# Load order and first matmuls of a fused linear-attention and SwiGLU kernel: x in two tiles, the first weight quarter in two halves, eight DMAs more

## The chip, the cores and the metric

The kernel runs on one core of one Trainium2 chip. The metric is the device time of one execution in microseconds (us). The program drives the TensorE matmul engine (PE in the profile), VectorE (DVE), ScalarE (ACT), GpSimd (POOL) and the queue of SyncE (SP), which issues nearly every DMA.

## What is computed

The input x has 2048 tokens of 512 numbers. Two blocks read it, and a gate per token mixes their results. Cut to what matters:

```python
g = sigmoid((x * gate_w).sum(-1, keepdims=True))
q, k, v = heads(x @ wqkv)                 # 32 heads of 16
pq, pk = phi(q), phi(k)                   # phi(t) = where(t > 0, t + 1, exp(t)) + 1e-6
kv = einsum("bhsd,bhse->bhde", pk, v);  z = pk.sum over tokens
a = (pq @ kv / (pq . z + 1e-6)) @ wo
b = (silu(x @ w1) * (x @ w3)) @ w2        # 1376 hidden columns
out = g * a + (1 - g) * b
```

All inputs and the output are bf16.

## The kernel before, in words

Tokens are worked in 16 tiles of 128 (`NT`), the 512 columns of x in four quarters of 128 (`kc`, `KC` = 4). A matmul contracts over 128 partitions, so a projection of one tile is four matmuls that add up in one PSUM bank, one for each quarter kc, and each needs the quarter kc of the weight and the transposed quarter of the tile, `xT[:, kc, tile]`.

**Loads.** They are issued from SP's queue (`dq`), in the order of the code, and SP issues one at a time. First comes `x_first` (L129): the first 256 tokens in one DMA of 256 KB, with two neighbouring tokens on each partition, so that tile 0 holds the even and tile 1 the odd tokens of the 256; `store` (L508) writes the output rows of tiles 0 and 1 back in the same pattern. Then `load_wqk(kc)` (L126) runs four times: each brings one quarter of wq and wk together, 256 KB. Then `load_xT(t)` (L123) brings tiles 2 to 15 already transposed, by DMA transposes; the same tiles untransposed (L141, named `natural`) come between them, in three DMAs. After those come gate and remainder columns (L143 to L147), w1 and w3 (L150, one DMA of 1280 KB each), wv (L151), wo (L152), w2 (L154) and w2x (L156). ACT's queue issues one small DMA, `touch` (L133).

**The first two tiles.** They are transposed on TensorE, by a matmul with the identity. The order is written out by hand. `warm_step(13)` (L359) runs 13 matmuls on constants. Then six transposes (L365) make quarters 0, 1 and 2 of both tiles; DVE (L379, L381) and ACT (L380, L382) copy them from PSUM into `xT`. The projections follow (`proj_mm`, L183): for quarter 0, k of tile 0, q of tile 0, k of tile 1 and q of tile 1, each in a bank of its own (banks 4 to 7); then the last two transposes (L365) and their copy (L394); the same four matmuls for quarter 1; k of both tiles for quarters 2 and 3; q of tile 0 and of tile 1 for quarters 2 and 3.

**What follows.** `phi` (ACT L196, DVE L198 and L201) turns a bank into pq or pk. `g_step` (L231) adds pk times x into four banks over all tokens; `k_step` and `q_step` project the next tiles. The sum of pk over all tokens is kept by POOL (L215), turned by a DMA transpose (`zaT`, L421) and spread over the partitions. Then four blocks of 512 tokens run through w1 and w3 (L303, L309), and the output tiles through L475 and L492.

Of the kernel before, what the change touches and what calls it, by code (L numbers as in the profile page):

```python
# [8 lines left out]
ACT = mybir.ActivationFunctionType  # L9
# [7 lines left out]
def kernel(  # L17
# [17 lines left out]
    nc = tc.nc  # L35
    P = nc.NUM_PARTITIONS

    Bb, S, D = A_x.shape
# [3 lines left out]
    KC = D // P  # L42
# [16 lines left out]
    x2d = A_x.flatten_outer_dims()  # L59
    out2d = out.flatten_outer_dims()  # L60
    x_t = x2d.rearrange("(t p) d -> p t d", p=P)
    wqkv_r = A_wqkv.rearrange("(kc d) n -> d kc n", d=P)
    w1_r = B_w1.rearrange("(kc d) f -> d kc f", d=P)
    w3_r = B_w3.rearrange("(kc d) f -> d kc f", d=P)
# [8 lines left out]
    ident = consts.tile([P, P], BF16, name="ident")  # L73
# [6 lines left out]
        out=bmask[:], in_=bmask[:], pattern=[[-Dh, HPC], [0, Dh]], compare_op=ALU.is_ge,  # L80
# [3 lines left out]
        out=bmask[:], in_=bmask[:], pattern=[[Dh, HPC], [0, Dh]], compare_op=ALU.is_ge,  # L84
# [22 lines left out]
    xN = consts.tile([P, NT, D], BF16, name="xN")  # L107
    wqk = consts.tile([P, KC, 2 * D], BF16, name="wqk")
    wq = wqk[:, :, 0:D]
    wk = wqk[:, :, D : 2 * D]  # L110
# [3 lines left out]
    w1 = consts.tile([P, KC, F0], BF16, name="w1")  # L114
    w3 = consts.tile([P, KC, F0], BF16, name="w3")
    w2 = consts.tile([P, FC, D], BF16, name="w2")
    xT = consts.tile([P, KC, S], BF16, name="xT")
    act_pre = consts.tile([P, 1], BF16, name="act_pre")
    dq = nc.sync
# [5 lines left out]
    def load_wqk(kc):  # L125
        dq.dma_start(out=wqk[:, kc, :], in_=wqkv_r[:, kc, 0 : 2 * D])  # L126

    x_first = x2d[0 : 2 * P, :].rearrange("(p j) d -> p j d", j=2)
    dq.dma_start(out=xN[:, 0:2, :], in_=x_first)  # L129
    nc.scalar.activation(out=act_pre[:], in_=warm[:, 0:1], func=ACT.Exp)  # L130

    touch = consts.tile([P, 2, 16], BF16, name="touch")
    nc.scalar.dma_start(out=touch[:], in_=wqkv_r[:, 1:3, 0:16])  # L133
    for kc in range(KC):
        load_wqk(kc)
    natural = {3: (2, 4), 5: (4, 8), 8: (8, 16)}
    for t in range(2, NT):
# [4 lines left out]
    with nc.allow_non_contiguous_dma(reason="gate column"):  # L142
        dq.dma_start(  # L143
            out=wr[:, :, 2 * FR : NR], in_=gate_w.rearrange("(kc d o) -> d kc o", d=P, o=1)
        )
    dq.dma_start(out=wr[:, :, 0:FR], in_=w1_r[:, :, F0:F])
    dq.dma_start(out=wr[:, :, FR : 2 * FR], in_=w3_r[:, :, F0:F])  # L147
    for w, w_r, cuts in ((w1, w1_r, (0, KC)), (w3, w3_r, (0, KC))):
        for a, b in zip(cuts, cuts[1:]):
            dq.dma_start(out=w[:, a:b, :], in_=w_r[:, a:b, 0:F0])  # L150
    dq.dma_start(out=wv[:], in_=wqkv_r[:, :, 2 * D : 3 * D])  # L151
# [5 lines left out]
        out=w2x[:].rearrange("p r d -> p (r d)"),  # L157
        in_=w2x_r[None].to_broadcast([TPB, RP, RG * D]),
# [11 lines left out]
    bank = [psum.tile([P, D], FP32, name=f"bank{i}") for i in range(8)]  # L170
    turn = {"mm": 0, "ab": 0}

    def mm_tile():
        turn["mm"] += 1
        return bank[4 + (turn["mm"] - 1) % 4]
# [6 lines left out]
    def proj_mm(ps, t, w, kc):  # L182
        nc.tensor.matmul(  # L183
            ps[:], lhsT=xT[:, kc, t * P : (t + 1) * P], rhs=w[:, kc, :],
            start=(kc == 0), stop=(kc == KC - 1),
        )
# [170 lines left out]
    def warm_step(n):  # L357
        for _ in range(n):
            nc.tensor.matmul(  # L359
                bank[7][:, 0:256], lhsT=warm[:, 0:P], rhs=warm, start=True, stop=True  # L360
            )

    def transpose_block(t, kc, dst):

        nc.tensor.matmul(  # L365
            dst, lhsT=xN[:, t, kc * P : (kc + 1) * P], rhs=ident[:], start=True, stop=True
        )

    def transpose_kc(kc, ps):
        for t in range(2):  # L370
            transpose_block(t, kc, ps[:, t * P : (t + 1) * P])

    warm_step(13)

    for t in range(2):
        transpose_block(t, 0, bank[t][:, 0:P])
    transpose_kc(1, bank[2])
    transpose_kc(2, bank[3])
    nc.vector.tensor_copy(out=xT[:, 0, 0:P], in_=bank[0][:, 0:P])  # L379
    nc.scalar.activation(out=xT[:, 0, P : 2 * P], in_=bank[1][:, 0:P], func=ACT.Copy)  # L380
    nc.vector.tensor_copy(out=xT[:, 1, 0 : 2 * P], in_=bank[2][:, 0 : 2 * P])  # L381
    nc.scalar.activation(out=xT[:, 2, 0 : 2 * P], in_=bank[3][:, 0 : 2 * P], func=ACT.Copy)  # L382
    first = {(t, n): mm_tile() for n, t in (("k", 0), ("k", 1), ("q", 0), ("q", 1))}
    w_of = {"k": wk, "q": wq}

    def first_mm(n, t, kc):
        proj_mm(first[t, n], t, w_of[n], kc)

    for kc in range(2):
        for n, t in (("k", 0), ("q", 0), ("k", 1), ("q", 1)):  # L390
            first_mm(n, t, kc)
        if kc == 0:
            transpose_kc(3, bank[0])
            nc.vector.tensor_copy(out=xT[:, 3, 0 : 2 * P], in_=bank[0][:, 0 : 2 * P])  # L394
    for kc in range(2, KC):
        for t in range(2):
            first_mm("k", t, kc)
# [103 lines left out]
        )  # L501

    def store(t, o, cs=slice(0, D)):
        if t < 2:
            rows = out2d[0 : 2 * P, :].rearrange("(p j) d -> p j d", j=2)[:, t, :]
        else:
            rows = out2d[t * P : (t + 1) * P, :]
        dq.dma_start(out=rows[:, cs], in_=o[:, cs])  # L508

    def out_first(tb):  # L510

        t = tb * TPB
        b_part(t, bank[0], range(AHEAD))
        rem_out_step(tb, bank, started=(0,))
        keep = [mm_tile() for _ in range(TPB)]
        rem_out_step(tb + 1, keep, ends=True)
        rem_keep(tb + 1, keep)
        b_part(t, bank[0], range(AHEAD, FC))
        aga = a_part(t, mm_tile())
        o = work.tile([P, D], BF16, tag="o", bufs=3, name="o")  # L520
        mix(t, bank[0], aga, o)
        store(t, o)

    def out_step(tb, tt):
        t = tb * TPB + tt
        held = tb % 2 == 0
        if held and tt == 0:
            return out_first(tb)
        aga = a_part(t, mm_tile() if held else ab_tile())
        o = work.tile([P, D], BF16, tag="o", bufs=3, name="o")  # L530
        if t < NT - 1:
            b_ps = bank[tt] if held else ab_tile()
            b_part(t, b_ps, range(FC), started=held)
            mix(t, b_ps, aga, o)
            store(t, o)
            return
        for lo, hi in ((0, 2 * P), (2 * P, 3 * P), (3 * P, D)):
            cs = slice(lo, hi)
            b_ps = ab_tile()
            b_part(t, b_ps, range(FC), cs)  # L540
            mix(t, b_ps, aga, o, cs)
            if lo == 0:
                store(t, o, cs)
        store(t, o, slice(2 * P, D))
# [56 lines left out]
```

## Time and profile before

| what | value |
|---|---|
| median of 3 runs | 178.08 us (178.05 to 178.58) |
| the profiled execution: its own time | 178.0 us |
| the profiled execution: its span, first to last instruction | 176.3 us |
| TensorE's granted clock, mean | 1.000 |
| PE busy | 172.5 us, 969 matmuls |
| DVE busy | 110.4 us |
| POOL busy | 63.2 us |
| ACT busy | 59.1 us |
| DMA | 15.57 MB, mean 88 GB/s |

All times inside the execution are counted from the start of the span; 1.7 us of the execution's own time lie outside it. "Busy" counts running instructions; issuing a DMA is not busy time. Neighbouring matmuls overlap, so a matmul of 128x512 lasts 379 ns but the next one starts some 216 ns after it: rows of the timeline give a group's first start and the time until its last end. A view that follows the chain of waits back from the last instruction tells which work set the end.

### The profile page before, as it was taken

What the parts mean: (1) busy time and instruction counts of PE and PEld (TensorE: products, weight loads), DVE (VectorE), ACT (ScalarE), POOL (GpSimd) and SP (SyncE); (2) the same over time, 40 slices, a digit from 0 to 9 for tenths busy, and PEclk for the clock granted to TensorE, in tenths of its full rate; (3) what the DMA queues carried; (4) which work ended last, traced back from release to release, by engine and by line L of the source; (5) the groups of instructions that cost most, each with busy time, mean ns of one, the idle gap of its engine ahead of it and who ended that gap; (6) DMA issues with size and microseconds to landing.
All of it is one profiled execution on the core that took longest, in us unless ns stands there. A gap on an engine that the chain in (4) does not pass through costs nothing.

```text
span 176.3 us, 2685 instructions
## 1 busy us (share of the span) xinstructions
PE 172.5 (98%) x969; PEld 82.5 (47%) x969; DVE 110.4 (63%) x207; ACT 59.1 (34%) x109; POOL 63.2 (36%) x106
## 2 busy tenths in 40 slices
PE   8999999999999999999999999999999999999993
PEld 5444444444456443444444466444444444444453
DVE  1399788888764899777343477853435775344363
ACT  4354544544753443422423101134225123422000
POOL 5086657557300668486400044550000562000000
DMA  6998959995204111323200013330000233000001
GB/s 186 262 178 228 183 103 279 402 349 198 66 4 52 26 30 34 83 65 89 60 0 0 0 33 84 84 89 0 0 4 0 60 89 89 4 0 0 30 30 60
DMA packets 29232, 15.57 MB, mean 88 GB/s; under 512 B 21028, under 2 KB 27428, under 8 KB 29220
## 3 DMA queue, kind: packets, MB, share of 16 engines
q1 hardware_dynamic: 28948, 15.41, 35.3%
q8 instruction: 7, 0.11, 0.3%
q10 hardware_dynamic: 272, 0.01, 0.1%
q14 instruction: 5, 0.04, 0.1%
HBM read 8.86 MB, written 2.10 MB: 62 GB/s over the span
## 4 chain that ended last, share of the span: by engine, by line
PE 94%; DMA 2%; SPq 1%; DVE 0%; issue 0%
PE bank L492 20%; PE bank L303 20%; PE bank L309 20%; PE bank L183 15%; PE bank L231 8%; PE bank L475 8%; PE bank L245 3%; DMA wqk<-in_A_wqkv_dram 2%; PE bank L278 2%; SPq L126 1%; PE bank L447 0%; SPq L129 0%; PE bank L462 0%; DVE o L498 0%
## 5 line engine op out<-in xcount | busy, mean ns | idle before, releaser
L315 DVE TENSOR_TENSOR hT<-bank,sg 128x512 bf16<-128x512 f32 x40 | 27.3, 682 | 31.0 <-PE bank L309 30.9
L303 PE MATMUL bank<-xT,w 128*128 128x512 bf16 x160 | 41.1, 379 | 0.0
L309 PE MATMUL bank<-xT,w 128*128 128x512 bf16 x160 | 41.1, 379 | 0.0
L314 ACT ACTIVATE sg<-bank 128x512 bf16<-128x512 f32 x40 | 23.9, 597 | 45.9 <-PE bank L303 45.9
L492 PE MATMUL bank<-w,hT 128*128 128x512 bf16 (+2 forms) x180 | 37.5, 355 | 0.0
L337 POOL TENSOR_TENSOR pqs<-pq,rden 128x512 bf16<-128x512 bf16 x16 | 16.9, 1056 | 54.4 <-issue 46.9
L183 PE MATMUL bank<-wqk,xT 128*128 128x512 bf16 x128 | 30.8, 381 | 0.1
L215 POOL TENSOR_TENSOR zacc<-zacc,pk 128x128 f32<-128x128 f32 x56 | 23.3, 446 | 10.4 <-DVE pk L201 10.4
L492 PEld LDWEIGHTS <-hT 128*128 128x128 bf16 x180 | 16.7, 98 | 18.4 <-issue 0.8
L309 PEld LDWEIGHTS <-w 128*128 128x128 bf16 x160 | 15.7, 98 | 18.9
L303 PEld LDWEIGHTS <-w 128*128 128x128 bf16 x160 | 15.5, 98 | 18.2 <-issue 0.2
L498 DVE SCALAR_TENSOR_TENSOR o<-bank,omg_all,aga 128x512 bf16<-128x512 f32 (+2 forms) x18 | 12.5, 692 | 14.6 <-PE bank L492 11.7
L183 PEld LDWEIGHTS <-xT 128*128 128x128 bf16 x128 | 12.4, 98 | 15.2 <-issue 0.7
L322 POOL TENSOR_TENSOR pr<-pq,zb 128x512 f32<-128x512 bf16 x16 | 18.4, 1154 | 0.1
L231 PE MATMUL bank<-pk,xN 128*128 128x512 bf16 x64 | 16.4, 379 | 0.0
L475 PE MATMUL bank<-M,pqT 128*128 128x512 bf16 x64 | 16.1, 379 | 0.0
L196 ACT ACTIVATE eq<-bank 128x512 bf16<-128x512 f32 x16 | 9.4, 597 | 16.0 <-PE bank L183 16.0
L201 DVE SCALAR_TENSOR_TENSOR pk<-bank,emk 128x512 bf16<-128x512 f32 x16 | 11.1, 692 | 1.6
L196 ACT ACTIVATE ek<-bank 128x512 bf16<-128x512 f32 x16 | 9.4, 597 | 6.7 <-PE bank L183 6.7
L201 DVE SCALAR_TENSOR_TENSOR pq<-bank,emq 128x512 bf16<-128x512 f32 x16 | 11.1, 692 | 0.5
L326 DVE TENSOR_REDUCE den<-pr 128x32 f32<-128x512 f32 x16 | 10.8, 676 | 0.0
L231 PEld LDWEIGHTS <-xN 128*128 128x128 bf16 x64 | 6.3, 98 | 7.6
(54 smaller groups left out, 95.7 us busy)
## 6 DMA issues: line engine op xcount, KB each, us to landing
w<-in_B_w_dram SPq DMA_DIRECT2D x3, 1280.0 KB, 10.2
out_dram<-o SPq DMA_DIRECT2D x15, 128.0 KB, 1.9
wqk<-in_A_wqkv_dram SPq DMA_DIRECT2D x4, 256.0 KB, 3.7
xN<-in_A_x_dram SPq DMA_DIRECT2D x1, 1024.0 KB
xN<-in_A_x_dram SPq DMA_DIRECT2D x2, 256.0 KB, 2.8
xN<-in_A_x_dram SPq DMA_DIRECT2D x1, 512.0 KB, 4.7
wv<-in_A_wqkv_dram SPq DMA_DIRECT2D x1, 512.0 KB, 11.2
wo<-in_A_wo_dram SPq DMA_DIRECT2D x1, 512.0 KB, 12.1
```

The costliest lines, as they stand in the source:

```text
L183: nc.tensor.matmul(ps[:], lhsT=xT[:, kc, t * P : (t + 1) * P], rhs=w[:, kc, :], start=(kc == 0), stop=(kc == KC - 1),)
L196: nc.scalar.activation(out=e[:], in_=ps[:], func=ACT.Exp)
L201: nc.vector.scalar_tensor_tensor(out=dst, in0=ps[:], scalar=0.0, in1=em[:], op0=ALU.max, op1=ALU.add)
L215: nc.gpsimd.tensor_tensor(out=(zaccb if t == NT - 1 else zacc)[:, cs], in0=zacc[:, cs], in1=pk[t][:, cs], op=ALU.add,)
L231: nc.tensor.matmul(bank[kc][:], lhsT=xN[:, t, kc * P : (kc + 1) * P], rhs=pk[t][:], start=(t == 0), stop=(t == NT - 1),)
L303: nc.tensor.matmul(g_ps[:], lhsT=w1[:, kc, fs], rhs=xT[:, kc, tok], start=(kc == 0), stop=(kc == KC - 1),)
L309: nc.tensor.matmul(u_ps[:], lhsT=w3[:, kc, fs], rhs=xT[:, kc, tok], start=(kc == 0), stop=(kc == KC - 1),)
L314: nc.scalar.activation(out=sg[:], in_=g_ps[:], func=ACT.Silu)
L315: nc.vector.tensor_tensor(out=hT[tb][:, fc, :], in0=u_ps[:], in1=sg[:], op=ALU.mult)
L322: nc.gpsimd.tensor_tensor(out=pr[t][:], in0=pq[:, t, :], in1=zb[:], op=ALU.mult)
L475: nc.tensor.matmul(ps[:], lhsT=pqT[:, c, ts], rhs=M2[:, c, :], start=(c == 0), stop=(c == KC - 1),)
L492: nc.tensor.matmul(ps[:, 0 : cs.stop - cs.start], lhsT=hT[tb][:, fc, tt * P : (tt + 1) * P], rhs=w2[:, fc, cs], start=(fc == 0 and not sta ...
```

## The change

x's first 256 tokens come in two DMAs of 128 KB, tile 0 being the first 128 tokens and tile 1 the next, and the first quarter of the weights in two, wk and wq; the issue order is x tile 0, wk's quarter 0, x tile 1, wq's quarter 0, then the joined quarters 1, 2 and 3 as before. w1 and w3 come in four DMAs each in place of one. These are eight DMAs more: one for x, one for the weight quarter, six for w1 and w3. There are 10 warm-up matmuls in place of 13. All four quarters of tile 0 are transposed first, one to a bank, and copied by DVE and ACT in turn in four copies; k of tile 0 for quarter 0 follows; then tile 1 is transposed into the same four banks and copied in the same way; then k of tile 1, q of tile 0 and q of tile 1 for quarter 0. Quarter 1 is projected in the order k 0, q 0, k 1, q 1; the rest has its order unchanged. The output rows of tiles 0 and 1 are stored as all others are.

```diff
-    x_first = x2d[0 : 2 * P, :].rearrange("(p j) d -> p j d", j=2)
-    dq.dma_start(out=xN[:, 0:2, :], in_=x_first)
+    def load_x(t):
+        dq.dma_start(out=xN[:, t, :], in_=x_t[:, t, :])
+
+    load_x(0)
...
-    for kc in range(KC):
+    dq.dma_start(out=wk[:, 0, :], in_=wqkv_r[:, 0, D : 2 * D])
+    load_x(1)
+    dq.dma_start(out=wq[:, 0, :], in_=wqkv_r[:, 0, 0:D])
+    for kc in range(1, KC):
         load_wqk(kc)
...
-    for w, w_r, cuts in ((w1, w1_r, (0, KC)), (w3, w3_r, (0, KC))):
+    for w, w_r, cuts in ((w1, w1_r, range(KC + 1)), (w3, w3_r, range(KC + 1))):
         for a, b in zip(cuts, cuts[1:]):
             dq.dma_start(out=w[:, a:b, :], in_=w_r[:, a:b, 0:F0])
...
-    def transpose_block(t, kc, dst):
...
-    def transpose_kc(kc, ps):
...
-    warm_step(13)
-
-    for t in range(2):
-        transpose_block(t, 0, bank[t][:, 0:P])
-    transpose_kc(1, bank[2])
-    transpose_kc(2, bank[3])
...
+    def transpose_tile(t):
+
+        ts = slice(t * P, (t + 1) * P)
+        for kc in range(KC):
+            nc.tensor.matmul(
+                bank[kc][:, 0:P], lhsT=xN[:, t, kc * P : (kc + 1) * P], rhs=ident[:],
+                start=True, stop=True,
+            )
+        for kc in range(KC):
+            if kc % 2 == 0:
+                nc.vector.tensor_copy(out=xT[:, kc, ts], in_=bank[kc][:, 0:P])
+            else:
+                nc.scalar.activation(out=xT[:, kc, ts], in_=bank[kc][:, 0:P], func=ACT.Copy)
+
+    warm_step(10)
+    transpose_tile(0)
...
-    for kc in range(2):
-        for n, t in (("k", 0), ("q", 0), ("k", 1), ("q", 1)):
-            first_mm(n, t, kc)
-        if kc == 0:
-            transpose_kc(3, bank[0])
-            nc.vector.tensor_copy(out=xT[:, 3, 0 : 2 * P], in_=bank[0][:, 0 : 2 * P])
+    first_mm("k", 0, 0)
+    transpose_tile(1)
+    for n, t in (("k", 1), ("q", 0), ("q", 1)):
+        first_mm(n, t, 0)
+    for n, t in (("k", 0), ("q", 0), ("k", 1), ("q", 1)):
+        first_mm(n, t, 1)
...
-        if t < 2:
-            rows = out2d[0 : 2 * P, :].rearrange("(p j) d -> p j d", j=2)[:, t, :]
-        else:
-            rows = out2d[t * P : (t + 1) * P, :]
-        dq.dma_start(out=rows[:, cs], in_=o[:, cs])
+        dq.dma_start(out=out2d[t * P : (t + 1) * P, cs], in_=o[:, cs])
```

More of the change, by code (lines that the diff above doesn't have):

```diff
@@ L361, in warm_step @@
             )
-    def transpose_block(t, kc, dst):
-        nc.tensor.matmul(
-            dst, lhsT=xN[:, t, kc * P : (kc + 1) * P], rhs=ident[:], start=True, stop=True
-        )
-    def transpose_kc(kc, ps):
-        for t in range(2):
-            transpose_block(t, kc, ps[:, t * P : (t + 1) * P])
-    warm_step(13)
-    for t in range(2):
-        transpose_block(t, 0, bank[t][:, 0:P])
-    transpose_kc(1, bank[2])
-    transpose_kc(2, bank[3])
[L379 to L382, printed above, removed]
+    def transpose_tile(t):
[12 more added lines that the diff above has]
+    transpose_tile(0)
     first = {(t, n): mm_tile() for n, t in (("k", 0), ("k", 1), ("q", 0), ("q", 1))}
```

## The prediction, made before the changed kernel ran

> **What bounds the kernel now.** I read part 1 of the page first. PE is busy for 172.5 of 176.3 us, so the time is PE's work plus the few places where PE waits.
>
> ```profile
> PE 172.5 (98%) x969; PEld 82.5 (47%) x969; DVE 110.4 (63%) x207; ACT 59.1 (34%) x109; POOL 63.2 (36%) x106
> ```
>
> Next comes the chain of work that ended last, in order of time (start, duration, what). Everything the change touches lies in its first 8 us.
>
> ```profile
> 0.80 0.39 SPq L129
> ...
> 2.19 0.43 SPq L126
> 2.62 0.04 issue
> 2.66 4.38 DMA wqk<-in_A_wqkv_dram
> 7.04 0.04 issue
> 7.08 2.32 PE bank L183 x10
> ```
>
> The chain does not run through x or the transposes. It runs through SP, which issues x and four weight quarters one after another, then through the landing of the fourth quarter at 7.04 us, and from 7.08 through PE to the end. What PE does before 7.08 counts only if it lasts beyond the landing. The timeline of the first 9 us, PE's rows and the weight loads' (PEld), shows how near it is:
>
> ```profile
> 0.84 2.93 PE L359 MATMUL bank<-const-bfloat16-1.0 128*128 128x256 bf16 x13 [0.84 <-PEq L585]
> 3.57 0.84 PE L365 MATMUL bank<-ident,xN 128*128 128x128 bf16 x6
> 3.92 0.29 DVE L379 CAST xT<-bank 128x128 bf16<-128x128 f32 x1 [3.92 <-PE bank L365]
> 4.26 1.26 PE L183 MATMUL bank<-wqk,xT 128*128 128x512 bf16 x4
> 5.36 0.28 PE L365 MATMUL bank<-ident,xN 128*128 128x128 bf16 x2
> 5.47 3.93 PE L183 MATMUL bank<-wqk,xT 128*128 128x512 bf16 x16
> 7.08 1.82 PEld L183 LDWEIGHTS <-xT 128*128 128x128 bf16 x9 [0.41 <-issue]
> ```
>
> Quarter 0 and all transposes are through at 5.47. Six matmuls follow at 0.216 us (an eight-matmul piece of the chain lasts 1.73 us): four for quarter 1, two for quarter 2. They would end at 6.77. The weight loads then stand still for 0.41 us until 7.08. So PE has some 0.3 us of slack before quarter 3, and no more than that can be won there.
>
> **The change, part by part.** The sum is made against the profiled execution's own 178.0 us (span 176.3); the median of the runs shown, 178.08, is 0.08 above it.
>
> *PE's start.* x's first tile is half the bytes of the old first load. That load landed 2.6 us after its issue (DMA issues of the profile), at 3.4. Half of it, 131 thousand bytes at the 335 GB/s quoted below, is 0.39 us, so tile 0 lands near 3.0. Ten warm-up matmuls end there too: 2.93/13 = 0.225 us each from 0.84 gives 3.1. Four transposes at some 0.11 us start there (say 3.05); the first copy starts 0.35 later (3.57 to 3.92 before) and lasts 0.29, and 0.05 passes to the matmul: 3.74, half a microsecond before the old 4.26. It takes 0.40 there (the first matmul of L183 started at 4.26, the second at 4.66), so tile 1's transposes run from 4.14 to 4.6, its first copy ends 0.64 after 4.14, and k of tile 1 starts near 4.83. Three matmuls at 0.216 end quarter 0 at 5.48, where it was 5.47. The early start is spent on a second round of transpose, copy and wait. Quarters 1 and 2 end at 6.78: nothing gained, nothing lost. The cover is quarter 3's landing. Without it each 0.1 us here would cost 0.1 us. The copies are two more (eight for six), on DVE and ACT, which have nothing else to do before 7.49.
>
> *The issue order.* SP's queue has these rows:
>
> ```profile
> 1.25 1.84 SPq L126 DMA_DIRECT2D wqk<-in_A_wqkv_dram  x4
> 3.14 2.59 SPq L123 DMA_TRANSPOSE xT<-in_A_x_dram  x2
> ```
>
> Four issues take 3.14 - 1.25 = 1.89, or 0.47 us each. Two more stand ahead of quarter 3, which is now issued at 2.66 + 0.94 = 3.60. What that does to the landing is the one term that counts, and the trace before cannot show it. Its ends: nothing, if the queue is full and the bytes alone decide, since x and the four quarters have the same 1.31 MB; +0.94, if the 4.38 us from issue to landing stays. Between them stands the rate of the transfers. Two stretches, the first of nearly only 2 KB packets (3.0 to 5.3 us), the second of 1 KB packets alone (11.0 to 11.9 us), columns packets, MB, share of 16 engines:
>
> ```profile
> DMA packets 451, 0.77 MB, mean 335 GB/s; under 512 B 75, under 2 KB 75, under 8 KB 451
> q1 hardware_dynamic: 421, 0.77, 102.9%
> ```
>
> ```profile
> q1 hardware_dynamic: 313, 0.32, 102.7%
> ```
>
> A 2 KB packet took 1.029 x 16 x 2.3/376 = 0.101 us of an engine (451 less the 75 small ones are 376), a 1 KB packet 1.027 x 16 x 0.9/313 = 0.047. Splitting rows costs nothing per byte. But a 128 KB load at every 0.47 us asks for 279 GB/s only, less than the 335 that the engines deliver: the first four loads now run at SP's pace, not the engines'. Data begin some 1.2 us after an issue (0.80 to about 2.0, where the DMA row of the first 9 us leaves zero). Quarter 1, issued at 2.66, therefore starts at 3.86, and the 786 thousand bytes of quarters 1 to 3 take 2.35 us at 335 GB/s, to 6.21. Before, 1.31 MB from 2.0 took to 5.91. That is +0.30. At 402 GB/s, the highest slice of the page, it is 3.86 + 1.96 = 5.82 against 5.26, or +0.56. I take the middle, **+0.43**, because the landing at 7.04 lies 1.1 us behind the flow's end, so some engines run late, and nothing shows that the new pauses absorb their lateness.
>
> *Behind quarter 3.* Tile 2's transposed load is issued 0.94 later too. It landed 4.4 us after 3.14, at 7.5, and its first matmul is PE's at 8.37 (six matmuls after 7.08). With the whole 0.94 it lands at 8.5, when PE would need it at 8.80: covered by 0.3. Tile 3 is needed 1.5 us later. POOL has no DMA in this queue.
>
> *w1 and w3 in quarters.* Six more issues of 0.51 us (L150) plus the 0.94 make SP 4.0 us later behind them; w2x, the last load, was issued by 36.6, and SP then waited 9.6 us for POOL's zaccb (SP's own waits) before it issued zaT at 46.4. The 5.6 us left cover it. w1 and w3 landed by 36.8, with first use at 46.5; wv by 38.3, first use 53.0. Price nothing; without the cover, up to 4.0 us. The stores keep their number and sizes: nothing.
>
> *Sum.* PE's start 0, issue order +0.43, the rest 0: 178.0 + 0.43 = 178.4, against the median 178.08 + 0.43 = **178.5 us**. Allowing the neighbourhood of the two rates, this case reaches from +0.2 to +0.7. A measurement of this kernel tells 0.3%, or 0.53 us, from no change: the case straddles that line.
>
> **The rivals.**
>
> *The landing goes by the issue, +0.7 to +0.94 (178.8 to 179.0).* For it: the first transposed load also landed 4.4 us after its issue, as quarter 3 did. Against it: the four quarters took 2.9, 3.2, 4.1 and 4.4, growing as a queue does.
>
> *The landing is no later, and PE moves up.* If what delayed quarter 3 was contention, with the transposes right behind it, a later issue of these and calmer first loads may bring it back to 7.04 or earlier. PE can use it to 6.8 only: -0.3 to +0.2, 177.8 to 178.3. For it: the 1.1 us between flow and landing. Against it: the fewer bytes in flight early on.
>
> *PE's clock comes up later (the slow side).* The page gives a mean granted clock of 1.000, but the rows show two speeds: six transposes in 0.84 us at 3.57, two in 0.28 at 5.36; matmuls 0.40 apart at 4.26, 0.216 from 4.93. The step follows some 4 us of unbroken PE work. The new order breaks it twice, each time from the end of four transposes to the first copied quarter, by 0.26 us. If that puts the step off until after quarter 2, nine matmuls (three, four, two) run at 0.43 from 4.83 and end at 8.7 instead of 7.08: +1.6, 179.7. It decides from a step later than about 6.8 us; earlier, the wait for quarter 3 hides it. Against it: PE stays busy for 87% of the time from 0.84 to 4.83 (0.52 of 3.99 idle), and 13 warm-ups or 10 plus transposes fill the same stretch. [...]
>
> **How the numbers follow.** Forecast 0.42 (0.27 within the line, 0.15 over it); landing by issue 0.24, all slower; landing no later 0.22, of which 0.04 are faster by over 0.3% and 0.18 within; late clock 0.10 slower; 0.02 for something else, slower. Faster 0.04, same 0.45, slower 0.51. The range 177.8 to 179.2 takes in the first three cases and leaves the late clock and the tails out; the forecast's own is 178.3 to 178.8.
>
> **What would show it.** In the profile after: SP issues quarter 3 near 3.6; its landing between 7.2 and 7.7, with PE's first matmul behind it and the idle time before it grown from 0.41 to 0.8 or so; the first projection at 3.7 and quarter 0 through near 5.5; no wait from there to the end, w1's first use included. A landing at 7.0 or before, a matmul spacing of 0.43 beyond 5 us, or a wait before tile 2's projection would each prove a step wrong.

## The result, and the profile after

The changed kernel takes 179.28 us (median of 18 runs, 178.57 to 180.79) and the kernel before 178.24 us (18 runs beside them, 177.66 to 178.90): a ratio of 1.0069, 95% interval 1.0048 to 1.0090. It is slower, by 1.0 us, more than the 0.4 forecast and just outside the range.

The profiled execution of the changed kernel lasts 178.86 us, 0.86 above that of before (178.0). Its span is 176.8, only 0.5 longer. So the loss has two parts, one inside the span and one outside. The chain of waits in order of time (start, duration, what), for the changed kernel:

```profile
0.80 0.39 SPq L129
...
2.67 0.43 SPq L126
3.10 0.04 issue
3.14 0.43 SPq L126
3.57 0.04 issue
3.61 3.95 DMA wqk<-in_A_wqkv_dram
7.57 0.04 issue
7.61 2.32 PE bank L188 x10
```

It has the shape it had before. SP issues seven loads in place of five, quarter 3 goes out at 3.61 instead of 2.66, lands at 7.57 instead of 7.04, and PE's dense stretch starts at 7.61 instead of 7.08: 0.53 later. From there on nothing changes. The issue of zaT, for instance, stands at 46.88 instead of 46.35, again 0.53 later. PE's rows in the timeline:

```profile
3.08 0.61 PE L372 MATMUL bank<-ident,xN 128*128 128x128 bf16 x4
3.76 0.61 PE L188 MATMUL bank<-wqk,xT 128*128 128x512 bf16 x1
4.16 0.63 PE L372 MATMUL bank<-ident,xN 128*128 128x128 bf16 x4
4.86 2.55 PE L188 MATMUL bank<-wqk,xT 128*128 128x512 bf16 x9
7.61 2.10 PE L188 MATMUL bank<-wqk,xT 128*128 128x512 bf16 x9 [0.20 <-DMA wqk<-in_A_wqkv_dram]
```

The first projection does start half a microsecond earlier (3.76 for 4.26). Then PE waits for tile 1's copy until 4.86. Inside the row of nine matmuls it also waits for quarter 2, which lands at 6.78 (the seventh of them ends near 6.5, the next starts at 6.82), and behind that row it waits for quarter 3.

The other 0.34 us lie outside the span: an execution's own time minus its span is 1.7 us before and 2.05 here, and it hardly varies within a kernel. The span does vary. Over the 18 runs it was 176.5 to 177.5 in thirteen and 178.0 to 178.7 in five, while the kernel before had 175.8 to 177.2 in all of its 72 runs whose span is known. The experiments take these three apart: the later landing, the long executions, and the time outside.

### The profile page after: what moved, and what is told of

It reads as the page before. It is cut to its first block, busy times and chain, and to the rows that moved or that the text cites. A ratio compares the mean times of both kernels' runs of the same rounds, so it can differ in the third digit from the quotient of the medians.

```text
span 176.8 us, 2672 instructions
## 1 busy us (share of the span) xinstructions
PE 171.5 (97%) x949; PEld 82.1 (46%) x966; DVE 109.8 (62%) x208; ACT 59.5 (34%) x111; POOL 63.2 (36%) x106
## 4 chain that ended last, share of the span: by engine, by line
PE 93%; DMA 2%; SPq 1%; issue 1%; DVE 0%
PE bank L308 20%; PE bank L493 20%; PE bank L314 19%; PE bank L188 15%; PE bank L236 8%; PE bank L476 8%; PE bank L250 3%; DMA wqk<-in_A_wqkv_dram 2%; PE bank L283 2%; SPq L126 0%; SPq L129 0%; PE bank L448 0%; SPq L138 0%; SPq L136 0%; PE bank L463 0%
## 5 line engine op out<-in xcount | busy, mean ns | idle before, releaser
L308 PE MATMUL bank<-xT,w 128*128 128x512 bf16 x158 | 40.8, 379 | 0.2
L314 PE MATMUL bank<-xT,w 128*128 128x512 bf16 x156 | 40.4, 379 | 0.1
L493 PE MATMUL bank<-w,hT 128*128 128x512 bf16 (+2 forms) x176 | 37.0, 355 | 0.5 <-issue 0.3
L476 PE MATMUL bank<-M,pqT 128*128 128x512 bf16 x61 | 15.6, 379 | 0.1
```

What stands on the lines that cost most here:

```text
L308: nc.tensor.matmul(g_ps[:], lhsT=w1[:, kc, fs], rhs=xT[:, kc, tok], start=(kc == 0), stop=(kc == KC - 1),)
L314: nc.tensor.matmul(u_ps[:], lhsT=w3[:, kc, fs], rhs=xT[:, kc, tok], start=(kc == 0), stop=(kc == KC - 1),)
L476: nc.tensor.matmul(ps[:], lhsT=pqT[:, c, ts], rhs=M2[:, c, :], start=(c == 0), stop=(c == KC - 1),)
L493: nc.tensor.matmul(ps[:, 0 : cs.stop - cs.start], lhsT=hT[tb][:, fc, tt * P : (tt + 1) * P], rhs=w2[:, fc, cs], start=(fc == 0 and not sta ...
```

## Experiments

Each kernel ran several times, with the kernel before on the same chip beside it. "Outside" is the median of time minus span, "ACT" and "DVE" the number of their instructions in part 1 of the page, "long" the runs whose span was over 177.9. The runs of the kernel before came in four sets, each beside some of the variants; their median span was 176.6 in three sets and 176.8 in the one beside the two queues, the two small loads, the two ACT more and the copies on DVE.

| kernel | time minus before, us | ratio, 95% interval | span, median | long | ACT / DVE | outside |
|---|---|---|---|---|---|---|
| before (72 runs) | | | 176.6 | 0 of 72 | 109 / 207 | 1.71 |
| changed | +1.04 | 1.0048 to 1.0090 | 177.2 | 5 of 18 | 111 / 208 | 2.05 |
| loads alone | +1.11 | 1.0061 to 1.0126 | 177.65 | 2 of 6 | 109 / 207 | 1.70 |
| changed, w1 and w3 whole | +1.17 | 1.0054 to 1.0110 | 177.4 | 2 of 6 | 111 / 208 | 2.04 |
| PE order alone | +0.47 | 1.0010 to 1.0035 | 176.7 | 0 of 12 | 111 / 208 | 2.04 |
| w1 and w3 in pieces alone | +0.21 | 1.0003 to 1.0032 | 176.8 | 0 of 12 | 109 / 207 | 1.70 |
| changed, two queues | +0.46 | 1.0022 to 1.0089 | 177.3 | 2 of 5 | 111 / 208 | 1.71 |
| before, two small loads | +0.67 | 1.0028 to 1.0121 | 177.5 | 2 of 5 | 109 / 207 | 1.71 |
| before, two ACT more | +0.39 | 1.0007 to 1.0040 | 176.9 | 0 of 5 | 111 / 207 | 2.03 |
| changed, copies on DVE | +0.42 | 1.0013 to 1.0070 | 177.1 | 1 of 5 | 109 / 210 | 1.86 |
| changed, two ACT more | +0.92 | 1.0046 to 1.0107 | 177.5 | 3 of 9 | 113 / 208 | 1.73 |
| changed, fillers | +1.14 | 1.0046 to 1.0084 | 177.35 | 0 of 6 | 111 / 208 | 2.04 |
| before, later need | +0.03 | 0.9984 to 1.0017 | 176.6 | 0 of 12 | 109 / 207 | 1.72 |
| before, few warm-ups | +1.04 | 1.0043 to 1.0093 | 177.6 | 2 of 7 | 109 / 207 | 1.71 |
| changed, fillers and two ACT | +0.60 | 1.0012 to 1.0042 | 177.2 | 0 of 8 | 113 / 208 | 1.73 |
| before, four ACT more | +0.15 | 1.0005 to 1.0025 | 176.8 | 0 of 9 | 113 / 207 | 1.71 |

### Which part carries what

**Loads alone.** The kernel before with the diff's edits to the loads of x and wqk and to the stores.

> The kernel before, with the new loads of x and of the first weight quarter in the new order, and the plain stores; 13 warm-ups, the old order of transposes and matmuls, w1 and w3 whole. Pacing theory (two more issues of 0.47 us on SP delay quarter 3 whatever PE does): quarter 3 lands near 7.57 us as in the changed kernel, PE's first matmul behind it starts near 7.6, the span is 0.5 us longer than before, 176.8. Rival, the new order on PE is what costs: landing may be late, but the span stays within 0.2 of 176.3 or the time does not move. Outside the span (1.7 us before, 2.05 in the changed kernel): if it grows with the number of DMAs, 2 more give about +0.1, so 178.8 to 178.9 in all; if it comes from the pieces of w1 and w3, it stays at 1.7.

The span grew by 1.05, more than expected, and the time outside stayed at 1.70. The chain of waits of this kernel:

```profile
3.62 4.54 DMA wqk<-in_A_wqkv_dram
8.16 0.04 issue
8.20 2.32 PE bank L188 x10
```

Quarter 3 landed at 8.16. The old order on PE is still there, so the loss inside the span belongs to the loads, and so do long runs. The stores, which this kernel changes too, are not the cause: 1.13 of the 1.3 us between the two profiled spans are there when zaT is issued (47.48 for 46.35), before the first store.

**PE order alone.** The diff's edits to transposes and first matmuls on the kernel before, with 13 warm-ups.

> The kernel before with the new order on PE alone (tile by tile transposes, eight copies, the new order of quarter 0), 13 warm-ups, the old loads and stores. Pacing theory: quarter 3 is issued at 2.66 and lands near 7.04 as before; PE starts from x at 3.4 instead of 3.0, so its own work to quarter 2 ends some 0.4 to 0.6 later than in the changed kernel, near 7.3 to 7.5, and now PE itself decides: span 0.2 to 0.5 above 176.3. Rival, late clock: in some runs one to two us more, as in five of the eighteen runs of the changed kernel (180.05 to 180.79). Outside the span 1.7 in both.

Quarter 3 landed at 6.92, and the chain shows that PE itself was the later of the two:

```profile
4.47 0.58 PE bank L183
5.06 0.10 PE bank L367
5.16 0.02 issue
5.18 0.30 DVE xT L373
5.49 0.05 issue
5.53 4.28 PE bank L183 x19
```

After the copy of tile 1's first quarter, nineteen matmuls run without a gap, through the place where quarter 3 is first needed. The span's median moved by 0.1 only, and no run was long; 0.33 of the loss of 0.47 is the time outside, 2.04.

**w1 and w3, both ways.** In the changed kernel:

```diff
-    for w, w_r, cuts in ((w1, w1_r, range(KC + 1)), (w3, w3_r, range(KC + 1))):
+    for w, w_r, cuts in ((w1, w1_r, (0, KC)), (w3, w3_r, (0, KC))):
```

and the reverse in the kernel before.

> The changed kernel with w1 and w3 loaded whole again, six DMAs fewer. Theory of a price for each DMA outside the span: time outside falls from 2.05 to about 1.8, the span stays at 176.8 to 177.0, the median falls by 0.25 to about 179.0. Pacing theory alone: no change, 179.3, since those loads are 9 us ahead of their first use. Rival, the pieces of w1 and w3 disturb the stream (a later landing, a slower z chain): the span itself falls.

> The kernel before with w1 and w3 in four loads each and nothing else. Price for each DMA outside the span: span 176.3 as before, time outside 1.7 + 0.25, median 0.2 to 0.3 above before. If nothing is paid for an issued DMA: median as before within 0.1. Rival, pieces disturb the stream: the span grows, by a wait at the first use of w1 or of the transposed z.

The price for each DMA falls: six more leave 1.70, six fewer leave 2.04. Undoing the pieces won nothing; making them cost 0.2, which is at the edge of what the runs can tell (0.05 to 0.6). In the profiled execution of that kernel 0.44 us of delay stand already at 9.84 (9.40 before), behind a wait for quarter 1 that landed at 6.09, while its first load of w1 is issued at 25.6; so that much, at least, is not the pieces' doing.

### The landing of quarter 3

**Two queues.** The changed kernel with

```diff
-    load_x(1)
-    dq.dma_start(out=wq[:, 0, :], in_=wqkv_r[:, 0, 0:D])
+    nc.scalar.dma_start(out=xN[:, 1, :], in_=x_t[:, 1, :])
+    nc.scalar.dma_start(out=wq[:, 0, :], in_=wqkv_r[:, 0, 0:D])
```

> The changed kernel, with x tile 1 and wq's quarter 0 issued from ACT's queue, where SP's issues do not wait for them: quarter 3 is again issued near 2.67. Landing goes by issue (some 4.4 us after it, whatever stands in the queue): landing near 7.1 instead of 7.6 to 8.1, span near 176.6 at the median (177.2 in the changed kernel). Flow theory (bytes at the engines' rate): the same bytes, no pauses between them, landing as before, also near 7.1. Rival, the smaller pieces themselves are slow (1 KB rows, more landings), wherever they are issued: span stays at 177.2 or more. Outside the span 2.05 as in the changed kernel if it goes with ACT's or PE's program.

Quarter 3, issued at 2.67, landed at 7.25, as expected. But the span did not come back (177.3, beside 176.8): in the profiled run, a long one, PE waited for wq's quarter 0 instead, which ACT's queue brought at 6.25, as the chain of waits shows (the three shorter runs, 177.1 to 177.3, have no profile):

```profile
1.85 4.40 DMA wqk<-in_A_wqkv_dram
6.25 0.04 issue
6.29 5.41 PE bank L188 x18
```

**Two small loads.** The kernel before with

```diff
+    small = consts.tile([P, 2, 16], BF16, name="small")
     for kc in range(KC):
+        if kc < 2:
+            dq.dma_start(out=small[:, kc, :], in_=wqkv_r[:, 3, kc * 16 : (kc + 1) * 16])
         load_wqk(kc)
```

> The kernel before, with two loads of 4 KB more on SP's queue, one ahead of quarter 0 and one ahead of quarter 1; nothing reads them. The same bytes of x and weights, in the old pieces, but quarter 3 is issued near 3.6. Landing goes by issue: landing near 8.0, span up by about 0.9 to 177.5. Flow theory: +0.3 to +0.56, span 176.9 to 177.1. Rival, the pieces are what costs (1 KB rows, splitting of x): nothing but the 4 KB, span 176.6 as before. Outside the span 1.70 in each case.

8 KB that nothing reads made the span 0.3 to 0.7 longer in the three shorter runs (177.1, 177.3, 177.5, beside a median of 176.8) and two of five long. So two issues ahead of quarter 3 are enough to cost span; smaller rows or more tiles are not needed to explain that. The size, 0.5 in the middle run, is nearer to the flow theory's +0.3 to +0.56 than to the +0.9 of a landing that goes by the issue, and the one profiled landing, 7.64, settles nothing: without the small loads, in the kernel with two ACT more beside it, quarter 3 landed at 7.62. Each of the two loads of 4 KB took as long on SP as a load of 256 KB, some 0.47 us: the first 0.41 and 0.05 to the next issue, the first quarter of the kernel before 0.42 and 0.05.

Put together: where quarter 3 was issued near 3.61, it landed at 7.57, 7.63, 7.64, 8.01, 8.07, 8.15, 8.15, 8.16, 8.27 and 8.29 in ten profiled executions, median 8.1. Where it was issued at 2.67, at 6.50, 6.92, 6.94, 7.04, 7.25, 7.48, 7.62 and 8.05, median 7.15. The medians differ by 0.95 and the means by 0.77, with an interval of some 0.4 to 1.2, since landings of one order spread so widely. The span moved less: in runs that are not long it lies 0.4 above that of the kernel before for the changed kernel, 0.25 to 0.75 for its variants, and 1.0 for loads alone.

Two more things stand in these eighteen traces. First, quarter 3 lands 0.67 to 0.79 us behind quarter 2 in every one, although it is issued 0.47 behind it; so what delays quarter 3 is there in quarter 2 already, and in five executions (w1 and w3 in pieces, two ACT more, four ACT more, copies on DVE, and one of the changed kernel) the chain runs through quarter 1, whose landing at 6.09 to 6.64 sets the start of sixteen matmuls. Second, a trace records sixteen completions for each load, and the load has landed with the last. With the old order in seven executions and the new one in nine (the two queues and the two small loads left aside), quarter 2's first completion came at 5.21 to 5.60 and at 5.79 to 6.06, medians 5.46 and 5.87: 0.41 later, although the issue is 0.95 later. Its last completion came 0.3 to 2.0 us behind the first with the old order (median 1.1) and 1.0 to 1.8 with the new one (median 1.5). So by these medians the first data of quarter 2 came 0.41 later, and the rest of the landing's move is a longer tail of late completions.

### The long executions

The two small loads' profiled execution is a long one (span 179.4). PE's rows:

```profile
3.57 0.84 PE L368 MATMUL bank<-ident,xN 128*128 128x128 bf16 x6
5.50 1.86 PE L186 MATMUL bank<-wqk,xT 128*128 128x512 bf16 x4 [1.09 <-DMA wqk<-in_A_wqkv_dram]
7.16 0.42 PE L368 MATMUL bank<-ident,xN 128*128 128x128 bf16 x2
7.38 4.34 PE L186 MATMUL bank<-wqk,xT 128*128 128x512 bf16 x13
```

PE stood idle for 1.09 us until quarter 0 came at 5.46. Four matmuls then take 1.86 where they took 1.26 before: they start 0.43 apart, and this lasts until 9.9, while quarter 3 had landed at 7.64. The clock's step is here, as in the prediction, the place where the spacing of matmuls falls from some 0.43 us (half speed) to 0.216 (full speed). The granted clock reads 1.00 on both sides of it (3.50 to 4.60 and 4.95 to 7.00 us of the kernel before), so that a clock is the cause is the author's reading and was not shown. In this execution the step came late, and PE, not the load, set the end. The profiled execution of two queues is a late clock too: after 6.29, matmuls start 0.43 apart until 8.80. PE's wait before that row was shorter, 0.48 us, behind one of 0.23 at 4.52.

```profile
6.29 3.04 PE L188 MATMUL bank<-wqk,xT 128*128 128x512 bf16 x7 [0.48 <-DMA wqk<-in_A_wqkv_dram]
```

A wait does not always do it. In loads alone PE waited 0.63 us for x's second tile, and the transposes behind that wait ran at full speed (they start 0.06 apart, where those at 3.57 in the kernel before start 0.11 apart):

```profile
4.52 0.45 PE L370 MATMUL bank<-ident,xN 128*128 128x128 bf16 x5 [0.63 <-DMA xN<-in_A_x_dram]
```

**Few warm-ups.** The kernel before with `warm_step(3)` for `warm_step(13)`; no load is touched.

> The kernel before with 3 warm-up matmuls in place of 13, so that PE is idle from about 1.5 to 3.45 us; the loads are untouched. Clock theory: full speed comes only after some 4 us of unbroken work, so not before about 7.5 to 8; transposes and the matmuls of quarters 0 and 1 run at half speed (0.43 apart), quarter 2 ends near 9.5, span 1.5 to 2.5 us longer, 178 to 179. Rival, the clock takes little notice of a pause of 2 us: step near 5, span 176.6 as before.

```profile
0.84 0.80 PE L359 MATMUL bank<-const-bfloat16-1.0 128*128 128x256 bf16 x3 [0.84 <-PEq L585]
3.59 0.82 PE L365 MATMUL bank<-ident,xN 128*128 128x128 bf16 x6 [1.94 <-DMA xN<-in_A_x_dram]
4.37 1.86 PE L183 MATMUL bank<-wqk,xT 128*128 128x512 bf16 x4
```

The same 1.86, after an idle stretch of 1.94 us; matmuls start 0.43 apart until 9.66, although quarter 3 landed early, at 6.50. Time +1.04. The size varies from run to run (spans 177.2 to 178.5), and five of seven are below what was expected.

**Fillers.** The changed kernel with

```diff
     transpose_tile(0)
+    warm_step(1)
...
     first_mm("k", 0, 0)
+    warm_step(2)
     transpose_tile(1)
-    for n, t in (("k", 1), ("q", 0), ("q", 1)):
+    warm_step(1)
+    first_mm("k", 1, 0)
+    warm_step(2)
+    for n, t in (("q", 0), ("q", 1)):
         first_mm(n, t, 0)
```

> The changed kernel with six more warm-up matmuls in the places where PE waits for a copy or a piece in quarter 0 (one behind each tile's transposes, two ahead of tile 1's, two behind k of tile 1). Clock theory (the runs of more than 178 us span come from a wait of PE of about a microsecond for a late piece, after which PE stays at half speed until 9 to 10 us): PE stays busy, no run above 177.8, median span near 177.0. Rival (those runs are late landings of quarter 3 as such): one run in four above 178 as before. The fillers take at most 6 x 0.21 us of PE ahead of a landing that comes 0.5 us after PE is ready, so a small loss is possible in the other runs: up to 0.4.

No run of six was long, nor one of eight in the kernel with fillers below. The changed kernel and all variants with the new loads, or two extra issues, and without fillers had 17 long runs in 54. The median span (177.35) did not fall: the landing still decides it.

**The changed kernel again, twice.** A single execution each.

> The changed kernel once more, for a profile of a run above 178 us of span (5 of 18 were). Clock theory: in such a run PE's matmuls are 0.43 us apart until 9 to 10 us, after a wait of about a microsecond for a late piece of quarter 0 or 1; span 178.0 to 178.7. Rival: matmuls 0.216 apart from 5 us on and a landing of quarter 3 near 9. A run below 178 should show the clock's step near 5 and a landing between 7.2 and 8.3.

> As the run before, a second execution of the changed kernel: late clock with matmuls 0.43 us apart until 9 to 10 us if the span is above 178, else a step near 5 and a landing of quarter 3 between 7.2 and 8.3.

Neither was long: spans 177.3 and 177.6, quarter 3 at 8.01 and 8.29, the step of the clock before 6 us in the first (matmuls start 0.40 and 0.38 apart from 5.01, then 0.216) and near 5.1 in the second. So a long execution of the changed kernel itself has no profile here; that its long runs are late clocks rests on its variant with two queues, on the two small loads and on the fillers. In the first of the two executions the chain ran through quarter 1:

```profile
2.67 3.98 DMA wqk<-in_A_wqkv_dram
6.64 0.04 issue
6.69 2.39 PE bank L188 x10
```

### The time outside the span

**Two ACT instructions more,** in the kernel before, then in the changed kernel; four more in the kernel before (128x1 each, near 2.3 us, when ACT is idle).

```diff
     nc.scalar.activation(out=act_pre[:], in_=warm[:, 0:1], func=ACT.Exp)
+    act_more = consts.tile([P, 2], BF16, name="act_more")
+    for i in range(2):
+        nc.scalar.activation(
+            out=act_more[:, i : i + 1], in_=warm[:, 0:1], func=ACT.Copy
+        )
```

> The kernel before with two more tiny ACT instructions (128x1) behind the first one, near 2.3 us, when ACT is idle. If the 0.34 us outside the span go with the two more ACT instructions of the new copies (111 for 109): outside 2.04, span 176.6 as before, median +0.3. Rival, they go with something else of the new order on PE: outside 1.70, no change of the median.

> The changed kernel with two more tiny ACT instructions near 2.3 us. So far 109 compute instructions on ACT (the kernel before) left 1.70 us outside the span, 111 left 2.04 (twice), 111 with two more DMA issues on ACT left 1.71. If the place where ACT's program ends decides, and not its length as such: outside 1.71 here, median 0.33 below the changed kernel's 179.28, near 178.95. If every two instructions cost 0.34: outside 2.4, median 179.6. Span as in the changed kernel, 177.2 at the median, with one run in four or so above 178.

> The kernel before with four more tiny ACT instructions. So far none more gave 1.70 us outside the span, two more 2.04, and the changed kernel with four more than before 1.73. If the time outside alternates with the length of ACT's program by two instructions: 1.70 here. If it depends on the whole program in a way that these runs do not show: 2.04 or another value.

**Copies on DVE.** The changed kernel with `if kc != 1` for `if kc % 2 == 0` in `transpose_tile`.

> The changed kernel with six of its eight copies on DVE and two on ACT, so that ACT has 109 instructions as in the kernel before and DVE 210. If the time outside the span goes with ACT's instructions: 1.70 outside, median 0.35 below the changed kernel. If it goes with DVE's or PE's program: 2.05 as it was. Span: the copies stay hidden behind quarter 3's landing, 177.2 at the median.

```profile
PE 171.5 (97%) x952; PEld 82.4 (47%) x969; DVE 110.9 (63%) x207; ACT 59.4 (34%) x111; POOL 63.3 (36%) x106
```

That is the kernel before with two more ACT instructions: 111, as in the changed kernel, and 2.03 outside. With four more it is 1.71 again, and two more in the changed kernel bring its 2.05 down to 1.73. So the 0.34 us come with two more ACT instructions, as the changed kernel's copies bring them, but not as work: two further instructions take them away. The copies on DVE, with ACT's count back at 109, gave 1.86 and not 1.70, and the kernel with two more DMA issues on ACT 1.71, so it is not ACT's count alone. What happens in that time no profile here shows.

### Putting it together, and a try at something better

**Fillers and two ACT** in the changed kernel, both edits above.

> The changed kernel with the six fillers on PE and the two tiny ACT instructions together. If the three parts are apart from each other (late clock, time outside the span, landing of quarter 3): outside 1.71, no run above 177.8 of span, median span 177.3, time 179.0, and what stays above the kernel before is the landing alone, 0.7. If the parts overlap, the runs above 178 come back or the outside is 2.04.

1.73 outside, no long run in eight, span 177.2: the parts add up. What is left, +0.60 (0.2 to 0.75), is the landing, 8.15 in the profiled execution, with whatever w1 and w3's pieces cost.

**Later need.** The kernel before, with

```diff
-    for kc in range(2, KC):
-        for t in range(2):
-            first_mm("k", t, kc)
+    for n, t in (("k", 0), ("k", 1), ("q", 0), ("q", 1)):
+        first_mm(n, t, 2)
+    for t in range(2):
+        first_mm("k", t, 3)
...
     k_step(2, bank[3])
+    k_step(3, bank[2])
...
+    g_step(0, range(2))
+    g_step(1, range(2))
+    q_step(2)
+    k_step(4)
+    g_step(0, range(2, KC))
+    g_step(1, range(2, KC))
```

> The kernel before, in which PE needs quarter 3 later: all four matmuls of quarter 2 come first, then quarter 3; k of tile 3 goes to bank 2 right behind k of tile 2, and what banks 2 and 3 gather for tiles 0 and 1 comes behind q of tile 2 and k of tile 4. The landing of quarter 3 sets the start of the dense stretch in the kernel before, at 7.25 us at the median, and PE is ready near 6.8: with two matmuls moved ahead it is ready near 7.2, so 0.43 us at most are won: span 176.2 at the median, time 177.9. Rival: the first pk is ready 2.1 us after its last matmul and PE's work in between is two matmuls shorter, or DVE falls behind: a new wait takes the gain, span 176.6 or more.

No difference (interval 0.9984 to 1.0017). In the profiled execution quarter 3 landed at 6.94 and PE reached it only at 7.58 (the clock's step came near 5.4), without a wait: the landing's cost had become PE's own. Nothing tried beats the kernel before.

## Why the prediction was wrong, point by point

The step that failed is the sum: it put the time outside the span at nothing more than before, and that time grew by 0.34. Less these 0.34 us, the 179.28 measured are 178.94, within the range. What remains is made of the landing, whose price of +0.43 was near for this kernel's shorter runs and low for most variants, and of late clocks in five runs of eighteen.

*PE's start* was right in mechanism and nearly in size: first projection 3.74 forecast, 3.76 measured; k of tile 1 at 4.83, measured 4.86. Quarter 0 ended at 5.65, not 5.48, since the clock's step fell on k of tile 1 (0.36 us to the next matmul, where 0.216 was forecast). Nothing was won, as forecast. Two details were off. The copies are three more, not two (eight for five: one more on DVE, two more on ACT), and the two on ACT are the ones that matter below. And quarter 2 was taken to be there when PE needs it: it landed at 6.78, so the weight loads stood still 0.43 us for it and 0.48 for quarter 3, where one pause of 0.8 was forecast.

*The issue order* was the right place. Its +0.43 was worked out from the flow of data, and if quarter 2's first completion is taken for that flow, it moved by 0.41 at the median: that part came true. The term had the late completions unchanged, "some engines run late, and nothing shows that the new pauses absorb their lateness"; they were not absorbed but came later still, by 0.4 at the median, so the landing moved by 0.95 (means 0.77). In span, the profiled execution has 0.53, the thirteen shorter runs of the changed kernel 0.4 (177.0 for 176.6), the two kernels with fillers 0.75 and 0.6, loads alone 1.0: +0.43 is at the low end. The rival "the landing goes by the issue" had the better price for the landing, but not the mechanism. Its constant 4.4 us from issue to landing does not show: quarters 1 to 3 of the changed kernel took 2.9, 3.6 and 3.95, still growing, as the argument against that rival said.

*The sum* failed at a term that it did not have. It took the 1.7 us outside the span for fixed, without a reason; they became 2.05. This third of the loss (0.34 of 1.04) is not the loads' (1.70 in loads alone), and no row of the profile before pointed to it. What happens in that time stays open; the runs show only that it changes with the instructions that ACT gets.

*The late clock* was priced at +1.6 with a chance of 0.10, as if it took all executions or none. It takes some: five of eighteen were 1.5 longer than the others (median span 178.5 against 177.0), which moves the median of the span from 177.0 to 177.2. The trigger named, two breaks of 0.26 us, was wrong: two breaks of 0.27 in the changed kernel's profile left the step near 5 us. Longer waits ahead of the step do it in some executions (1.94, 1.09 and 0.48 us above) and not in others (0.63), so the wait's length alone does not decide. The step also varies without a wait. In four ACT more PE worked from 0.84 on without a wait in its rows and was still at half speed at 5.97 (two transposes 0.11 apart). In w1 and w3 in pieces alone it was at full speed by 3.58, six transposes in 0.52 us:

```profile
3.58 0.52 PE L365 MATMUL bank<-ident,xN 128*128 128x128 bf16 x6
```

So "some 4 us of unbroken PE work", read off one execution, is no rule here: full speed was there 2.7 us after PE's first matmul (0.84) in this run, and came 6.1 us after PE resumed at 3.59 in few warm-ups and some 4.5 us after it resumed at 5.50 in the two small loads. What sets the step was not shown.

*Behind quarter 3, w1 and w3, the stores*: right. Tile 2 landed at 8.19 and was needed at 8.90; the dense stretch has no new wait. A cost of w1 and w3's pieces is not shown; in the profile of their run the delay is there before they are issued.

## What to carry to other kernels

Where the first dense stretch waits for the last of a row of loads, count the issues ahead of that load: each took 0.47 us of SP here, two of them moved quarter 2's first completion by some 0.4 us and the landing by more, and splitting a load to start something earlier pays only if that something is on the chain. Early work that leaves PE idle before the step of its clock can cost more than it wins: 1.94 us of idling there (few warm-ups) went with 1.04 us more of time, and the changed kernel's five long runs were 1.5 us longer than the others. And compare an execution's time with its span before explaining a difference of a few tenths.

## What was not expected of the hardware

Time outside the span depends on the program's make-up: 109, 111 and 113 ACT instructions in otherwise equal kernels gave 1.71, 2.03 and 1.71 us, constant to about 0.1 within each. Landings of one and the same load, in the same place of the queue, spread over 1.5 us between executions (6.50 to 8.05 for quarter 3); the late ones follow late last completions of quarters 1 and 2, and why these come late stays open.
